# An attention and spectral-mixing kernel on one core: the weights of its issue planner set per quarter of a chunk instead of per chunk

## The chip, the core and the metric

The kernel runs on one core of one Trainium2 chip. Times are device microseconds (us) of that core. Three runs of the kernel before took 399.91, 400.09 and 401.86 us; their median is 400.09 us. The engines are called as in the profile: PE (matmuls) with PEld (its weight loads), ACT, DVE, POOL, and SP, which only issues DMAs here.

## The reference

Softmax attention over 2048 tokens (16 heads of 28) and a two-dimensional Fourier filter are computed of the same input and mixed by a gate per token.

```python
def reference(A_x, A_wqkv, A_wo, B_x, B_w_r, B_w_i, gate_w):
    def _A_ref(x, wqkv, wo):                       # x: 1 x 2048 x 448
        q, k, v = qkv[0], qkv[1], qkv[2]           # 16 heads of 28
        scores = jnp.einsum("bhqd,bhkd->bhqk", q, k) * Dh ** -0.5
        p = _softmax(scores, axis=-1)
        o = jnp.einsum("bhqk,bhkd->bhqd", p, v)
        return o.transpose(...).reshape(B, S, D) @ wo
    def _B_ref(x, w_r, w_i):
        X = jnp.fft.rfft2(x.astype(jnp.float32), axes=(-2, -1))
        y = jnp.fft.irfft2(X * (w_r + 1j * w_i), s=(S, D), axes=(-2, -1))
        return y.astype(jnp.bfloat16)
    x = A_x
    g = _sigmoid((x * gate_w).sum(-1, keepdims=True))
    a = _A_ref(x, A_wqkv, A_wo)
    b = _B_ref(x, B_w_r, B_w_i)
    return g * a + (1 - g) * b
```

## The kernel before

**The attention.** The 16 heads form four groups G of four heads; the 2048 queries form four blocks j of 512. A pair (G, j) is a *chunk*, and there are 16. Inside a chunk the keys come in 16 blocks of 128. One such block for the four heads of the group is a *pack*: 16 packs a chunk, 256 in all. Each pack needs four score matmuls (`KT` by `QT`, 128 keys x 512 queries each), an exponential of each, and four matmuls by the values (`Vb`) that add into the one PSUM bank `psV`.

**Two ways for a pack.** On the ACT way the scores go into the double banks `psA` and `psB`, two heads at a time; that pair is called a *score tile* here. ACT turns a score tile into `P` with one exponential of 128x1024 (L901), so an ACT pack takes two of them. `P` is a ring of 20 slots of 512 columns, which is ten exponentials; the first five ACT packs go into `VS` instead (`nearly=5`). On the DVE way each head's scores go into a bank `psX`, DVE turns them into the bits of an approximate exponential by an add and a maximum (L930), and three shifted copies of 128x2048 (L936) refine it; the pack then takes four passes of value matmuls instead of one. So an ACT pack costs ACT two instructions, and a DVE pack costs DVE seven.

**The rest.** Around this stream stand the projections of keys, queries and values, the norms that bound the scores (`sq`, `brow`, which goes into `QT` by DMAs), the gate (`glog`, `ge`, `gg`), the Fourier stages (`f1`, `f2`, `f3`, `i1`, `i2` by their unit names, over `UZ`, `P2`, `FX`, `t`, `Qf`), the division of each chunk by its sums (`osb`, `rs`, `rg`, `RB`, then a product on POOL, L1521) and the output projection (`out`). At the start the weights of group 0's values are exponentiated on ACT (L1227) and multiplied into `Vb` on DVE (L1348) before any value matmul may run.

**The planner.** Nothing of the order is written out by hand. `Plan.run` holds a clock for each engine and gives the engine that is furthest behind its next piece of work; the emitted program follows that order, engine by engine, and the engines then run in order with semaphores between them. For PE, `pe_step` first issues the next score tile if its bank pair is free; otherwise every other piece that is ready makes an `offer` with a score, and the lowest wins. Terms of the score are the weights: `w_pv` (value matmuls), `w_open` and `w_new` (units of background work), `w_d` (scores for a DVE pack), `w_due`, `w_late`, `w_hungry`, `sw_pen` (a change between row-tiled and column-tiled matmuls). `tol` is how late a score tile may become; `z_hard` and `z_soft` say at which PE load filler matmuls (`zero`) are added; `d_open`, `ahead`, `sh_max` and `d_urg` steer how many packs DVE claims. `step` does the same for DVE, ACT, POOL and SP by priority. Which pack goes to ACT and which to DVE falls out of this.

Progress is `next_a / 16`, the index of the next unclaimed pack in chunks, from 0 to 16, and 17 when no scores are left. The planner looks up its weights by progress.

```python
        self.cfgs = [dict(cfg, **cfg["seg"].get(i, {})) for i in range(18)]
...
            self.cfg = self.cfgs[int(self.progress())]
...
        if not any(self.s_left):
            return 17.0
        return (self.next_a if self.next_a < self.NP else self.NP) / 16.0
```

Of the kernel before, what the change touches and what calls it, by code (L numbers as in the profile page):

```python
# [111 lines left out]
class Op:  # L112
# [46 lines left out]
class Plan:  # L159
# [116 lines left out]
    def run(self):  # L276
        c = self.cfg
        self.mode = "full"
        self.owner = {b: None for b in self.banks}
        self.free_at = {b: 0.0 for b in self.banks}  # L280
        self.port_until = {"DVE": 0.0, "POOL": 0.0}
        self.marks = getattr(self, "marks", {})
        self.cells = []
        for o in self.ops:
            self.register(o)
        for u in self.units:
            for o in u.pe:
# [552 lines left out]
    def unit_run(self, u, o, t):  # L840
# [3 lines left out]
        self.pe_run(o, t)  # L844


CFG = dict(
    port_dep=6.0, last=((0, 2), (2, 2)), x_act=4, tiles=(2, 2), nring=20, nvar=10, nearly=5, l_pe=0.09, l_act=0.03, pe_lat=0.2, dma_issue=0.6,
    m_pe=0.2, m_bank=0.1, tol=0.1, max_ahead=9, nd_max=99, d_open=3, ahead=3, d_chunks=1, dve_op1=0.605, dve_shift=0.6, pool_shift=2.0,
    pool_shifts=(), pool_every=0, prio_op1=3, prio_shift=2.5, sh_max=4, d_urg=2, window=3.413, z_hard=3450, z_soft=3500, v2_at=2.0, v2_due=2.8,  # L850
    g_at=(0.9, 4.3, 8.0), g_due=1.0, w_pv=1.0, w_open=0.5, w_new=1.6, w_late=0.5, w_d=3, w_due=2, hungry=1.4, v_rush=2, x_rush=6, k_rush=5, q_rush=4,
    w_hungry=1, sw_pen=0, pv_min=1, ring_urg=2, d_first=True,
    seg={
        0: dict(d_open=4, w_hungry=0, z_hard=3550, w_open=1.2),
        1: dict(tol=0),
        3: dict(tol=0.15),
        4: dict(ahead=2, tol=0.15),
        5: dict(v2_due=3.1, hungry=4, w_pv=0.6, tol=0.15),
        6: dict(hungry=4, prio_shift=3, tol=0.15),
        7: dict(w_pv=0.6, tol=0, v2_at=0.5, prio_shift=3),  # L860
        8: dict(w_pv=0.6, tol=0, prio_shift=3, z_hard=3550),
        9: dict(d_urg=1, d_chunks=0, w_due=4, prio_shift=3, z_hard=3550),
        10: dict(z_hard=3550, d_open=4),
        11: dict(z_hard=3550, g_at=[1.1, 4.3, 8.0]),
        12: dict(d_urg=1, ring_urg=8, z_hard=3550),
        13: dict(ring_urg=4, w_pv=0.2, prio_shift=3, z_hard=3550, d_urg=1, w_new=2.0, z_soft=3800, w_late=2),
        14: dict(w_open=0.2, prio_shift=3.5, ahead=1, w_late=2, w_pv=0.2, ring_urg=4, w_new=2.0, w_due=4, pv_min=2, z_soft=3800),
        15: dict(prio_shift=3.5, w_open=0.2, w_late=1, w_pv=0.2, z_hard=3350, w_new=1.2, w_due=4, pv_min=2, z_soft=3800),
        16: dict(sw_pen=1.5),
        17: dict(z_soft=3800, w_new=1.2),  # L870
    },
)

# [69 lines left out]
class Kernel:  # L943
# [36 lines left out]
    def tiles(self, ctx):  # L980
# [629 lines left out]
```

## Time and profile before

| | |
|---|---|
| median of three runs | 400.09 us |
| the profiled execution | 400.49 us |
| its span, first to last instruction | 398.7 us |
| granted PE clock over the span | 1.000 |
| POOL busy | 126.9 us (32%) |
| DMA, mean over the span | 44 GB/s, 17.69 MB |

The span is 1.79 us shorter than the time of the same execution. In the profile's rows a column holds the start, the length, the engine, the line of the program, the operation, `out<-in`, the shapes and the count; what stands in brackets is idle time before it and what ended it. A score tile and its exponential carry the same number in the text: exponential 21 reads score tile 21.

### The profile page before, as it was taken

What the parts mean: (1) busy time and instruction counts of PE and PEld (TensorE: products, weight loads), DVE (VectorE), ACT (ScalarE), POOL (GpSimd) and SP (SyncE); (2) the same over time, 40 slices, a digit from 0 to 9 for tenths busy, and PEclk for the clock granted to TensorE, in tenths of its full rate; (3) what the DMA queues carried; (4) which work ended last, traced back from release to release, by engine and by line L of the source; (5) the groups of instructions that cost most, each with busy time, mean ns of one, the idle gap of its engine ahead of it and who ended that gap; (6) DMA issues with size and microseconds to landing.
All of it is one profiled execution on the core that took longest, in us unless ns stands there. A gap on an engine that the chain in (4) does not pass through costs nothing.

```text
span 398.7 us, 12653 instructions
## 1 busy us (share of the span) xinstructions
PE 386.0 (97%) x5221; PEld 134.9 (34%) x5221; DVE 344.3 (86%) x622; ACT 383.6 (96%) x424; POOL 126.9 (32%) x176
## 2 busy tenths in 40 slices
PE   8999999999999999999999999999999999999996
PEld 4444332223333322332332333333334332323233
DVE  3668999988887897898799797799998999999992
ACT  4898999999999999999999999999999999999993
POOL 1044214432333135525444534542436720101010
PEclk9999999999999999999999999999999999999999
DMA  8800022000121102120130112012100100001012
GB/s 250 181 31 5 2 28 58 13 19 3 37 70 34 40 3 66 32 77 20 24 100 19 56 37 58 14 42 74 36 29 2 29 3 25 30 27 50 26 53 71
DMA packets 24394, 17.69 MB, mean 44 GB/s; under 512 B 15731, under 2 KB 19744, under 8 KB 24336
## 3 DMA queue, kind: packets, MB, share of 16 engines
q1 hardware_dynamic: 23728, 16.69, 15.7%
q8 instruction: 41, 0.67, 0.7%
q10 hardware_dynamic: 608, 0.19, 0.3%
q14 instruction: 17, 0.14, 0.1%
HBM read 14.71 MB, written 1.97 MB: 42 GB/s over the span
## 4 chain that ended last, share of the span: by engine, by line
PE 46%; ACT 44%; issue 8%; DMA 1%; DVE 1%; ACTq 0%; DVEq 0%
ACT P L901 44%; PE psX L952 16%; PE psV L952 13%; PE psB L952 8%; PE psA L952 8%; DMA xtok<-in_A_x_dram 1%; PE psX L1202 1%; ACT VS L901 0%; DVE KT L1246 0%; DVE QT L1246 0%; ACT Vb L1227 0%; DVE Vb L1348 0%; PE psV L1202 0%; ACT sq L1556 0%; ACT sq L1237 0%
## 5 line engine op out<-in xcount | busy, mean ns | idle before, releaser
L901 ACT ACTIVATE P<-psB 128x1024 bf16<-128x1024 f32 x198 | 219.9, 1110 | 0.0
L901 ACT ACTIVATE P<-psA 128x1024 bf16<-128x1024 f32 x198 | 219.6, 1109 | 0.1
L930 DVE TENSOR_SCALAR VS<-psX 128x512 int16<-128x512 f32 x212 | 138.9, 681 | 17.3 <-PE psX L952 16.4
L936 DVE TENSOR_SCALAR VS<-VS 128x2048 int16<-128x2048 int16 x159 | 101.5, 689 | 0.4
L952 PEld LDWEIGHTS <-KT 32*128 32x128 bf16 (+1 forms) x1040 | 47.8, 91 | 145.3 <-issue 141.0
L952 PE MATMUL psB<-QT,KT 32*128 32x512 bf16 x406 | 79.2, 382 | 6.3 <-ACT P L901 5.0
L952 PE MATMUL psA<-QT,KT 32*128 32x512 bf16 x406 | 79.6, 383 | 0.9 <-DVE QT L1246 0.6
L952 PE MATMUL psV<-VS,Vb 128*32 128x512 bf16 x868 | 76.0, 385 | 0.1
L952 PE MATMUL psV<-P,Vb 128*32 128x512 bf16 x792 | 73.7, 385 | 0.0
L952 PE MATMUL psX<-QT,KT 32*128 32x512 bf16 x212 | 70.4, 383 | 0.0
L952 PEld LDWEIGHTS <-Vb 128*32 128x32 bf16 x1660 | 33.3, 94 | 57.0 <-issue 51.9
L1441 POOL TENSOR_TENSOR t<-FX,Wf 128x452 bf16<-128x452 f32 x32 | 31.8, 1013 | 56.1 <-PE psX L952 26.3
L1521 POOL TENSOR_TENSOR xtok<-osb,RB 128x512 bf16<-128x512 f32 x12 | 15.3, 1274 | 61.8 <-DMA RB<-rgd 47.6
L1184 POOL TENSOR_TENSOR sq<-QT 128x512 bf16<-128x512 bf16 x16 | 16.6, 1040 | 42.9 <-DVE QT L1266 17.3
L1495 POOL TENSOR_TENSOR UZ<-tab 128x225 bf16<-128x225 f32 (+1 forms) x32 | 17.7, 583 | 21.0 <-DVE VS L936 14.7
L952 PE MATMUL psX<-xT,Wk 112*32 112x512 bf16 x256 | 20.5, 383 | 0.0
L952 PE MATMUL psX<-xT,Wq 112*32 112x512 bf16 x240 | 20.0, 383 | 0.0
L1184 POOL TENSOR_TENSOR sq<-KT 128x512 bf16<-128x512 bf16 x12 | 12.5, 1040 | 22.6 <-DVE KT L1174 17.1
L952 PE MATMUL psX<-Bd,UZ 112*32 112x452 bf16 x256 | 19.6, 358 | 0.0
L1449 POOL TENSOR_TENSOR t<-t,t 128x226 bf16<-128x226 bf16 x32 | 17.9, 584 | 5.0 <-DVE VS L936 4.3
L952 PE MATMUL psX<-Wv,xT 112*32 112x113 bf16 (+1 forms) x512 | 19.4, 262 | 0.0
L952 PEld LDWEIGHTS <-xT 112*32 112x32 bf16 (+1 forms) x576 | 10.5, 96 | 9.0 <-issue 7.0
(105 smaller groups left out, 301.5 us busy)
## 6 DMA issues: line engine op xcount, KB each, us to landing
tab<-c_tab SPq DMA_DIRECT2D x16, 256.0 KB
RB<-rgd SPq DMA_DIRECT2D x60, 64.0 KB
xtok<-in_A_x_dram SPq DMA_DIRECT2D x4, 448.0 KB
out_dram<-ost SPq DMA_DIRECT2D x6, 224.0 KB
rs<-osb SPq DMA_DIRECT2D x60, 2.0 KB
Wf<-in_B_w_r_dram SPq DMA_DIRECT2D x31, 28.1 KB
Wf<-in_B_w_i_dram SPq DMA_DIRECT2D x31, 28.1 KB
Qf<-in_A_wqkv_dram SPq DMA_DIRECT2D x2, 294.0 KB
```

Of the source, the lines that this page charges most:

```text
L901: k.nc.scalar.activation(out=out, in_=k.psS[e["grp"]][:, 0:n, :], func=ACT.Exp, scale=LN2_128)
L930: k.nc.vector.tensor_scalar(out=k.VS[:, slot, 512 * h:512 * h + 512], in0=bank, scalar1=float(BITS0), scalar2=BITS_MIN, op0=ALU.add, op1=A ...
L936: k.nc.vector.tensor_scalar(out=k.VS[:, dst, :], in0=k.VS[:, src, :], scalar1=float(SHIFTS[v - 1]), scalar2=None, op0=ALU.add)
L952: self.nc.tensor.matmul(out, lhsT=lhsT, rhs=rhs, start=start, stop=stop, skip_group_check=True, **kw)
L1184: (self.nc.vector if e == "DVE" else self.nc.gpsimd).tensor_tensor(out=sq[:, :], in0=src, in1=src, op=ALU.mult)
L1202: nc.tensor.transpose(out=bb[0:C, 512 * ci + 128 * k:512 * ci + 128 * k + 128], in_=self.xtok3[:, 4 * b + k, C * c:C * c + C], identity=se ...
L1441: ts.append(pl.op("POOL", 1.07, lambda e, i=i, q=q: nc.gpsimd.tensor_tensor(out=self.t12[i][q][:, :].rearrange("p (r f) -> p r f", r=2), i ...
L1449: (nc.vector if e == "DVE" else nc.gpsimd).tensor_tensor(out=t1[:, FP * q:FP * q + FP], in0=t1[:, FP * q:FP * q + FP], in1=t2[:, FP - FP * ...
L1495: nc.gpsimd.tensor_tensor(out=z, in0=a, in1=b, op=ALU.subtract if q else ALU.add)
L1521: prev = pl.op("POOL", 1.3, lambda e, G=G, j=j: nc.gpsimd.tensor_tensor(out=self.ON[G][:, 512 * j:512 * j + 512], in0=self.osb[:, :], in1= ...
```

## The change

`GRAIN = 4` cuts each chunk into four quarters of four packs. The table of weights has 72 entries in place of 18, and each quarter has its own. Most entries of before are spread over their four quarters with further weights added.

```diff
-        self.cfgs = [dict(cfg, **cfg["seg"].get(i, {})) for i in range(18)]
+        self.cfgs = [dict(cfg, **cfg["seg"].get(i, {})) for i in range(18 * GRAIN)]
...
-            self.cfg = self.cfgs[int(self.progress())]
+            self.cfg = self.cfgs[int(GRAIN * self.progress())]
...
+GRAIN = 4
...
-        0: dict(d_open=4, w_hungry=0, z_hard=3550, w_open=1.2),
-        1: dict(tol=0),
-        3: dict(tol=0.15),
...
-        10: dict(z_hard=3550, d_open=4),
-        11: dict(z_hard=3550, g_at=[1.1, 4.3, 8.0]),
...
-        16: dict(sw_pen=1.5),
-        17: dict(z_soft=3800, w_new=1.2),
+        0: dict(d_open=4, w_hungry=0, z_hard=3550, w_open=1.2, tol=0.15, sh_max=3),
+        1: dict(d_open=4, w_hungry=0, z_hard=3350, w_open=1.2, tol=0.15, sh_max=3, w_late=4, w_d=2.2),
+        2: dict(d_open=4, w_hungry=0, z_hard=3550, w_open=1.2, tol=0.15, sh_max=3, prio_shift=3),
+        3: dict(d_open=4, w_hungry=0, z_hard=3550, w_open=1.2, ahead=6, max_ahead=5),
+        4: dict(tol=0),
...
+        40: dict(d_open=4, hungry=3, d_urg=3, sw_pen=0.25, pv_min=3),
+        41: dict(z_hard=3550, d_open=4, hungry=3, d_urg=3, sw_pen=0.25, pv_min=3),
+        42: dict(z_hard=3550, d_open=4, hungry=3, sw_pen=0.25, pv_min=3, w_new=2.0, w_due=0, ahead=2),
+        43: dict(z_hard=3550, d_open=4, hungry=3),
+        44: dict(z_hard=3550, g_at=[1.1, 4.3, 8.0], hungry=0, w_due=0.5, prio_shift=3.5),
...
+        68: dict(z_soft=3800, w_new=1.2, z_hard=3350, pv_min=3),
+        69: dict(z_soft=3800, w_new=1.2, z_hard=3350, pv_min=3),
+        70: dict(z_soft=3800, w_new=1.2, z_hard=3350, pv_min=3),
+        71: dict(z_soft=3800, w_new=1.2, z_hard=3350, pv_min=3),
```

The functions that emit instructions are the same, and every line below the table of weights moves by 56 (L901 becomes L957). What the planner makes of the new weights is seen in the two built programs, engine by engine. The counts that differ:

| instructions | before | after |
|---|---|---|
| ACT exponentials of score tiles (L901) | 406 | 404 |
| DVE bits of a head's scores (L930) | 212 | 216 |
| DVE shifted copies (L936) | 159 | 162 |
| value matmuls, four to a pass, from `P` / from `VS` | 792 / 868 | 788 / 884 |
| filler matmuls, four to a pass, into `psV` / `psX` | 8 / 12 | 32 / 0 |
| stretches of one tiling mode on PE | 787 | 794 |
| evacuation of key block 1 of group 0 (L1244, L1246) | DVE | ACT |
| one DMA queue (SP) and POOL: instructions by kind | same | same |

So one pack of 256 goes from ACT to DVE. Places in the order, counted in score tiles issued on PE or exponentials issued on ACT before them:

| place | before | after |
|---|---|---|
| ACT squares of key blocks of group 0 (L1237) | after exponentials 2, 6, 10 | 2, 4, 5 |
| ACT exponential of the value weights (L1227) | after 19 | after 14 |
| ACT exponential of the gate (L1358) | after 20 | after 26 |
| last of the first four value units on PE | tile 21 | tile 25 |
| first value matmuls from `VS` / from `P` | tile 21 / 22 | tile 18 / 20 |
| first scores of a DVE pack | tile 22 | tile 16 |
| `psV` evacuated, chunks 0 to 14, first and last | tile 33, 387 | tile 30, 383 |
| last `i1` and first `i2` | tile 295, 302 | tile 293, 295 |
| last scores of a DVE pack | 2 tiles before the last | 7 tiles before the last |

More of the change, by code (lines that the diff above doesn't have):

```diff
@@ L864 @@
-        11: dict(z_hard=3550, g_at=[1.1, 4.3, 8.0]),
[L865 to L868, printed above, removed]
-        16: dict(sw_pen=1.5),
@@ new lines @@
+        7: dict(tol=0, d_urg=0, pv_min=2),
+        8: dict(d_urg=0, z_hard=3550, w_pv=1.4),
+        9: dict(d_urg=3, hungry=1, w_new=2.4),
+        10: dict(sw_pen=2, ahead=1),
+        11: dict(pv_min=2),
+        12: dict(tol=0.15, pv_min=2, z_soft=4200, ring_urg=10),
+        13: dict(tol=0.15, pv_min=2, z_soft=4200, ring_urg=10, ahead=1),
+        14: dict(tol=0.15, pv_min=2, z_soft=4200, ring_urg=10, ahead=1),
+        15: dict(tol=0.15, pv_min=2, z_soft=4200, ring_urg=10, sh_max=2),
+        16: dict(tol=0.15, pv_min=2, z_soft=4200, ring_urg=10),
@@ new lines @@
+        17: dict(ahead=1, tol=0.15, pv_min=2, z_soft=4200, ring_urg=10, sw_pen=1),
+        18: dict(ahead=2, tol=0.15, pv_min=2, z_soft=4200, ring_urg=10, w_pv=1.8),
+        19: dict(ahead=2, tol=0.15, pv_min=2, z_soft=4200, ring_urg=10, w_pv=1.8, w_d=1, prio_shift=3.5),
+        20: dict(v2_due=3.1, hungry=4, w_pv=1.8, tol=0.15, ring_urg=10, w_d=1, prio_shift=3, sh_max=3),
+        21: dict(v2_due=3.1, hungry=4, tol=0.15, w_d=1, prio_shift=3.5, w_hungry=0, z_soft=4200),
+        22: dict(v2_due=3.1, hungry=3, w_pv=0.6, tol=0.15, w_d=1, prio_shift=3.5, z_soft=4200, d_first=False, d_urg=3),
@@ new lines @@
+        23: dict(v2_due=3.1, hungry=4, w_pv=0.6, tol=0.15, w_d=1, prio_shift=3.5, z_soft=4200, d_first=False, d_urg=3, w_due=4, ahead=4),
+        24: dict(hungry=4, tol=0.15, w_d=1.7, z_soft=4200, d_first=False, d_urg=3, w_due=4, ahead=4, sw_pen=2, w_new=0.8),
+        25: dict(hungry=4, prio_shift=3.5, tol=0.06, w_d=1, z_soft=4200, d_first=False, d_urg=3, w_due=4, ahead=4, pv_min=3, ring_urg=6),
+        26: dict(hungry=4, prio_shift=3.5, tol=0.15, w_d=1, z_soft=4200, d_first=False, d_urg=3, w_due=4, ahead=4),
@@ new lines @@
+        27: dict(hungry=4, prio_shift=3.5, tol=0.15, w_d=1, z_soft=4200, d_first=False, d_urg=3, w_due=4, ahead=6, ring_urg=10),
+        28: dict(w_pv=0.6, tol=0, v2_at=0.5, prio_shift=3, z_soft=4200, d_first=False, hungry=3, d_urg=3, ring_urg=10, ahead=6),
+        29: dict(w_pv=0.6, tol=0, v2_at=0.5, z_soft=4200, hungry=3),
+        30: dict(w_pv=0.6, tol=0, v2_at=0.5, prio_shift=3, z_soft=4200, d_first=False, hungry=3, d_urg=3, w_due=0),
+        31: dict(w_pv=0.6, tol=0, v2_at=0.5, prio_shift=3, z_soft=4200, d_first=False, hungry=1, d_urg=3),
@@ new lines @@
+        32: dict(w_pv=0.6, prio_shift=3, z_soft=4200, d_first=False, hungry=1, d_urg=3, sw_pen=0.25),
+        33: dict(w_pv=0.6, prio_shift=3, z_soft=4200, hungry=1, d_urg=3, sw_pen=2),
+        34: dict(w_pv=0.6, prio_shift=3, z_soft=4200, hungry=3, d_urg=3, sw_pen=2, w_late=2),
+        35: dict(w_pv=0.6, prio_shift=3, hungry=3, d_urg=3, sw_pen=0.25),
+        36: dict(d_urg=3, d_chunks=0, w_due=4, prio_shift=3, hungry=4, sw_pen=0.25, w_new=0.8, w_hungry=2),
+        37: dict(d_urg=3, d_chunks=0, w_due=4, prio_shift=3, hungry=3, sw_pen=0.25, max_ahead=5),
@@ new lines @@
+        44: dict(z_hard=3550, g_at=[1.1, 4.3, 8.0], hungry=0, w_due=0.5, prio_shift=3.5),
+        45: dict(z_hard=3550, g_at=[1.1, 4.3, 8.0], hungry=0, w_due=0.5, prio_shift=3.5, sw_pen=0.25),
+        46: dict(z_hard=3550, g_at=[1.1, 4.3, 8.0], sw_pen=0.5),
+        47: dict(z_hard=3550, g_at=[1.1, 4.3, 8.0], sw_pen=0.25, d_first=False),
+        48: dict(d_urg=1, ring_urg=8, z_hard=3550, sw_pen=0.5, w_new=2.4),
+        49: dict(d_urg=1, ring_urg=8, z_hard=3250, sw_pen=0.5),
+        50: dict(d_urg=1, ring_urg=8, z_hard=3250, sw_pen=0.5),
@@ new lines @@
+        51: dict(d_urg=1, ring_urg=8, z_hard=3550, sw_pen=0.5, z_soft=4200, ahead=5, pv_min=3),
+        52: dict(ring_urg=4, w_pv=0.2, prio_shift=3, z_hard=3550, d_urg=1, w_new=2.4, z_soft=4200, ahead=5, pv_min=3),
+        53: dict(ring_urg=4, w_pv=0.2, prio_shift=3, z_hard=3550, d_urg=1, w_new=2.4, z_soft=4200, ahead=5, pv_min=3, w_d=0.5, hungry=2),
+        54: dict(ring_urg=4, w_pv=0.2, prio_shift=3, z_hard=3550, d_urg=1, w_new=2.4, z_soft=3800, w_d=0.5, ahead=5, hungry=2, d_first=False),
@@ new lines @@
+        55: dict(ring_urg=4, w_pv=0.2, prio_shift=3, z_hard=3550, d_urg=1, w_new=2.4, z_soft=3800, w_late=2, tol=0, sh_max=1),
+        56: dict(w_open=0.2, prio_shift=3.5, ahead=1, w_late=2, w_pv=0.2, ring_urg=4, w_new=2.4, w_due=4, pv_min=2, z_soft=3800, z_hard=3350),
+        57: dict(prio_shift=3.5, ahead=1, w_late=2, w_pv=0.2, ring_urg=4, w_new=2.0, w_due=4, z_soft=3800, z_hard=3350, d_urg=0),
+        58: dict(prio_shift=3.5, ahead=1, w_late=2, w_pv=0.2, ring_urg=4, w_new=2.0, w_due=4, z_soft=3800, z_hard=3350, d_urg=0),
```

19 lines of the change are left out of this document (13 added, 6 removed).

## The prediction

> **What bounds the kernel now.** I read the page first: its table of engines, then the chain.
>
> ```profile
> span 398.7 us, 12653 instructions
> PE 386.0 (97%) x5221; PEld 134.9 (34%) x5221; DVE 344.3 (86%) x622; ACT 383.6 (96%) x424; POOL 126.9 (32%) x176
> ...
> PE 46%; ACT 44%; issue 8%; DMA 1%; DVE 1%; ACTq 0%; DVEq 0%
> ```
>
> PE and ACT look equally full and the chain passes between them, so neither view says which sets the pace. The groups, and then the exponentials from number 21 on as instructions of one line, do.
>
> ```profile
> L901 ACT ACTIVATE P<-psA 128x1024 bf16<-128x1024 f32 x198 | 219.6, 1109 | 0.1
> L952 PE MATMUL psB<-QT,KT 32*128 32x512 bf16 x406 | 79.2, 382 | 6.3 <-ACT P L901 5.0
> L901 ACT ACTIVATE P<-psA x193: 1017/1105/1290, 34.7 to 387.3; 128x1024 bf16<-128x1024 f32 x193
> L901 ACT ACTIVATE P<-psB x193: 1017/1098/1292, 35.6 to 388.2; 128x1024 bf16<-128x1024 f32 x193
> ```
>
> ACT is almost never idle before an exponential, while PE waits 5.0 us for ACT before score tiles. The timeline of ACT gives the pace.
>
> ```profile
> 12.65 1.02 ACT L901 ACTIVATE VS<-psA 128x1024 bf16<-128x1024 f32 x1 [1.10 <-PE psB L952]
> ...
> 14.96 1.04 ACT L901 ACTIVATE VS<-psA 128x1024 bf16<-128x1024 f32 x1
> ...
> 17.67 1.08 ACT L901 ACTIVATE VS<-psB 128x1024 bf16<-128x1024 f32 x1
> 18.57 0.67 ACT L1237 ACTIVATE sq<-psX 128x512 bf16<-128x512 f32 x1
> 19.05 1.10 ACT L901 ACTIVATE VS<-psA 128x1024 bf16<-128x1024 f32 x1
> ...
> 30.41 1.23 ACT L901 ACTIVATE P<-psA 128x1024 bf16<-128x1024 f32 x1
> 31.33 0.65 ACT L1227 ACTIVATE Vb<-psX 128x64 bf16<-128x64 f32 x1
> 31.44 1.40 ACT L901 ACTIVATE P<-psB 128x1024 bf16<-128x1024 f32 x1
> 34.35 0.21 ACT L1358 ACTIVATE ge<-glog 128x16 f32<-128x16 f32 x1 [1.51 <-DVE glog L1334]
> 34.71 1.02 ACT L901 ACTIVATE P<-psA 128x1024 bf16<-128x1024 f32 x1
> ...
> 388.22 1.04 ACT L901 ACTIVATE P<-psB 128x1024 bf16<-128x1024 f32 x1
> ```
>
> From 14.96 to 17.67 are three steps of 0.903 (the durations overlap): call 0.905 the floor. From exponential 21 (34.71) to 406 (388.22) the 385 steps take 353.51, or 0.918 each, 1.4% above the floor: ACT bounds this stretch. So the span is a sum along ACT: 12.65 to the first exponential, 22.06 for 20 steps, 353.51 for 385, 1.04 for the last, 9.44 behind it (398.70 - 389.26). At the floor the 20 steps would take 18.10. Three squares among them cost 0.475 each (17.67 to 19.05 is 1.38), together 1.43. The step from 31.44 is 3.27, or 2.37 too long. The 0.16 left is mostly L1227, whose step is 1.03.
>
> What that step of 3.27 waits for stands on PE and DVE.
>
> ```profile
> 33.03 0.39 PE L952 MATMUL psB<-QT,KT 32*128 32x512 bf16 x2
> ...
> 33.35 1.05 PE L952 MATMUL psV<-VS,Vb 128*32 128x512 bf16 x16
> 34.23 1.25 PE L952 MATMUL psV<-P,Vb 128*32 128x512 bf16 x20
> ...
> 32.02 1.70 DVE L1348 TENSOR_TENSOR Vb<-Vb 128x448 bf16<-128x448 bf16 x3 [1.22 <-ACT Vb L1227]
> ...
> 34.16 0.15 DVE L1334 COPY glog<-psX 128x4 f32<-128x4 f32 x1
> ```
>
> Two things are late at once. Exponential 21 is the first to overwrite a slot of the ring, so the ring's first pack must have had its value matmuls; those start at 34.23, behind tile 22, since `Vb` is weighted only from 32.02 on, right behind L1227. And the gate's exponential, placed ahead of 21, waits for `glog`, which leaves DVE at 34.16 behind the same work.
>
> **The change part by part, along that sum.**
>
> *Until the first exponential: 0.* One more group of 8 transposes stands ahead of score tile 1, where PE waits 0.58 us for a DVE result whose place does not change, and takes the place of a filler:
>
> ```profile
> 12.23 0.39 PE L952 MATMUL psA<-QT,KT 32*128 32x512 bf16 x2 [0.58 <-DVE QT L1246]
> ```
>
> *The first 20 steps: -1.65 with the gate's exponential.* The squares cost ACT the same 1.43 wherever they stand. L1227 moves from behind exponential 19 to behind 14: 12.65 + 14 x 0.905 + 1.43 + 0.48 (the added evacuation, below) = 27.2 in place of 31.33. DVE starts weighting 0.69 later as before (32.02 - 31.33), at 27.9, and by its order does five more pieces of up to 0.6 until the second weighting is done, at 30.3 at most. The first matmuls from `P` stand behind tile 20; its bank comes free with exponential 18, at 31.0, and a change of mode (33.03 to 33.35: 0.32) and three passes of 0.22 (33.35 to 34.23: four in 0.88) end near 32.2. Exponential 21 is due near 32.8 (12.65 + 18.10 + 1.43 + 0.48 + 0.12): 0.6 to spare. The gate's exponential now stands behind 26, at 38.2 or later; the last `glog` follows value matmuls behind tile 25, whose bank comes free at 35.5; with the change of mode, the matmuls and two pieces on DVE that is about 37.1. Both are then in time, by 0.6 and 1.1 us, and I see nothing that is late next; the 2.37 goes. The gate's exponential itself still costs something: at least what L1227 costs its step (1.03 - 0.905 = 0.12), at most 0.36 (34.35 to 34.71). So 2.01 to 2.25, and I take 2.13.
>
> Against it: one key block's evacuation (L1244, an Identity of 128x512 from PSUM) moves to ACT. No Identity runs on ACT in this trace; the nearest row is the square of the same shape, 0.475, and I take 0.48. It is 0 if ACT would have waited for tile 5 anyway, and 0.67, the square's whole duration, if nothing overlaps it. DVE loses the same work. 2.13 - 0.48 = 1.65.
>
> The Trainium skill (ScalarE: Activation LUTs, section What ACT_TABLE_LOAD costs) says that each per-partition pointer operand of an activation adds about 93 ns, and this Identity has such a bias where the square has none. By that rule it would cost 0.57 and the part 1.56. No row of before shows it.
>
> *Two exponentials fewer: -1.84.* 2 x 0.918; 1.81 at the floor. The pack they leave goes to DVE:
>
> ```profile
> L936 DVE TENSOR_SCALAR VS<-VS 128x2048 int16<-128x2048 int16 x159 | 101.5, 689 | 0.4
> 387.06 1.90 DVE L936 TENSOR_SCALAR VS<-VS 128x2048 int16<-128x2048 int16 x3
> ```
>
> Three shifts span 1.90, so one occupies (1.90 - 0.69) / 2 = 0.60; seven instructions (a bits instruction counted alike) are 4.2 us of DVE, which was busy 344.3 of 398.7. PE gains three passes of value matmuls, three of fillers and seven changes of mode at 0.10 (0.32 - 0.22): 0.66 + 0.66 + 0.70 = 2.0. Summing every pass of the built orders at such steps, 20 score tiles carry at most 18.15 us of PE work before and 18.19 after, against 18.36 for 20 exponentials, so ACT covers it; without that cover it costs the 2.0.
>
> *The other 383 steps: 0.* Their excess of 0.013 a step is spread evenly. A calm and a busy stage bound it:
>
> ```profile
> L901 ACT ACTIVATE P<-psA x20: 1051/1086/1237, 181.6 to 216.3; 128x1024 bf16<-128x1024 f32 x20
> ...
> L901 ACT ACTIVATE P<-psB x20: 1017/1025/1067, 329.2 to 364.3; 128x1024 bf16<-128x1024 f32 x20
> ```
>
> 38 steps take 34.7 (0.913) in one and 35.1 (0.924) in the other: over 383 steps -1.9 or +2.1. I take no change, since the PE work per 20 tiles is alike. Each ring slot is released with at least one tile to spare in the new order; before, only the stall above had less. On SP the same DMAs stand nearly in the same order: of group 1's four `QT` rows three now stand behind one store of `rg`, with 14 score tiles until they are read (17 before). POOL's work is the same.
>
> *Behind the last exponential: 0.*
>
> ```profile
> 389.43 0.39 PE L952 MATMUL psV<-P,Vb 128*32 128x512 bf16 x4
> ```
>
> The last pass starts 0.17 after that exponential ends, and what follows it is the same list. The DVE packs end earlier in the order, which can free 0.1 at most.
>
> **Sum.** -1.65 - 1.84 = -3.49. Against the profiled execution, 400.49 (span 398.70 and 1.79 around it): 397.0. That execution stood 0.40 above the median of the runs shown, so for the median 400.09 - 3.49 = 396.6.
>
> **Rivals.** *The stall moves (398.7).* If `glog` or the ring is late again, the 2.13 stays: -1.84 + 0.48 = -1.36. For: it was a wait on hardware that the order did not foresee; against: the margins of 0.6 and 1.1 us above.
>
> *DVE takes over in a stretch (398.4).* Counted at 0.60 a piece, the new order gives DVE 37.4 us of work over score tiles 260 to 300 (32.7 before), where 40 exponentials need 36.7. If PE then waits for DVE packs, the moved pack returns its 1.8. Against: from tile 260 to the end DVE has 124.5 us of work in 132.2, so the backlog of 0.7 clears.
>
> *Late evacuations of `psV` (405.6, the slower side).* One bank takes all value matmuls, and each chunk's first must wait for one DVE copy:
>
> ```profile
> L1512 DVE COPY osb<-psV 128x512 f32<-128x512 f32 x15 | 10.2, 679 | 0.0
> ```
>
> With DVE fuller, each of the 15 may queue behind one more piece of 0.60 with PE at a standstill: +9.0, so 400.09 - 3.49 + 9.0. From 10 such delays on the kernel is over 0.5% slower. Against: most ring slots leave five tiles or more of slack, and DVE's fullest stages before show no gap on ACT.
>
> *PE's clock drops (403.6).* It is 1.00 throughout:
>
> ```profile
> PEclk9999999999999999999999999999999999999999
> ```
>
> At half clock a pass takes 0.43 for 0.22, and 20 score tiles with 16 us of PE work need some 25, about 7 more than ACT: -3.49 + 7. The emptiest four tiles hold the columns of 3456 full-array cycles before (tile 288) and 3594 after (tile 351), so nothing gets emptier. The Trainium skill (TensorE: Matmul & The Clock Gate, Part 1) says that an idle window of about 3.4 us halves the clock; nothing here has shown one.
>
> *The middle tightens (394.7).* All steps as in the calm stage: -1.9.
>
> **How the numbers follow.** The forecast, 395.0 to 398.0 as its own range, gets 0.55; the stall moved 0.13; DVE's stretch 0.10; late evacuations 0.08; the clock 0.04; the tighter middle 0.10. Over 0.5%, 2.0 us, counts as a difference, so faster means under 398.1: 0.55 + 0.10 + half of DVE's case = 0.70. Same: 0.13 + 0.05 = 0.18. Slower: 0.12. The range 394.7 to 400.0 leaves out those 0.12 and the lower half of the tighter middle, 0.05.
>
> **What would show it.** 404 exponentials, the last ending near 385.8 in a span near 395.2; exponential 21 at 32.8 with no step over 1.5 us behind it; a mean step of 0.918 from there; 9.4 us behind the last. An idle ACT ahead of `ge` or 21 shows the first rival, DVE rows without gaps with PE waiting for them the second, gaps of PE ahead of value matmuls ended by `osb` the third. I am wrong if the mean step leaves 0.913 to 0.924.

## The result, and the profile after

The changed kernel takes **397.78 us** (median of ten runs, 397.10 to 399.75); beside it the kernel before took 400.64 us (ten runs, 399.91 to 402.34). The ratio is 0.9934, with an interval of 0.9911 to 0.9958: faster by about 2.6 us. The forecast was 396.6 us with 395.0 to 398.0 as its own range. The profiled execution took 397.11 us with a span of 395.3.

The page of the changed kernel, its span, its engines and its chain of waits:

```profile
span 395.3 us, 12706 instructions
PE 384.1 (97%) x5244; PEld 131.4 (33%) x5244; DVE 347.0 (88%) x628; ACT 382.7 (97%) x423; POOL 127.5 (32%) x176
...
PE 51%; ACT 39%; issue 7%; DVE 1%; DMA 1%; SPq 0%; DVEq 0%; ACTq 0%
```

Both engines stay at 97%, but the chain has shifted: before it ran 46% over PE and 44% over ACT, now 51% and 39%. The steps of ACT that run long are more: behind exponential 21, 18 of them exceed 1.0 us, where before 10 did. The groups and the exponentials out of `psB` from number 20 on, as instructions of one line, give the rest:

```profile
L1008 PE MATMUL psB<-QT,KT 32*128 32x512 bf16 x404 | 78.6, 383 | 4.2 <-ACT P L957 3.4
L957 ACT ACTIVATE P<-psB x193: 1017/1086/1292, 31.6 to 385.3; 128x1024 bf16<-128x1024 f32 x193
```

PE waited 5.0 us for ACT ahead of score tiles in `psB` before, and 3.4 us now. The timeline of ACT in the changed kernel (start, length, engine, line, operation) has the places that the prediction named:

```profile
12.13 1.02 ACT L957 ACTIVATE VS<-psA 128x1024 bf16<-128x1024 f32 x1 [1.09 <-PE psB L1008]
13.05 1.02 ACT L957 ACTIVATE VS<-psB 128x1024 bf16<-128x1024 f32 x1
...
14.43 1.04 ACT L957 ACTIVATE VS<-psA 128x1024 bf16<-128x1024 f32 x1
15.34 1.06 ACT L957 ACTIVATE VS<-psB 128x1024 bf16<-128x1024 f32 x1
16.24 0.72 ACT L1300 ACTIVATE KT<-psX,onef 128x512 bf16<-128x512 f32 x1
...
17.29 1.08 ACT L957 ACTIVATE VS<-psA 128x1024 bf16<-128x1024 f32 x1
...
31.60 1.28 ACT L957 ACTIVATE P<-psB 128x1024 bf16<-128x1024 f32 x1
32.68 1.12 ACT L957 ACTIVATE P<-psA 128x1024 bf16<-128x1024 f32 x1
...
37.34 1.05 ACT L957 ACTIVATE P<-psB 128x1024 bf16<-128x1024 f32 x1
38.26 0.22 ACT L1414 ACTIVATE ge<-glog 128x16 f32<-128x16 f32 x1
38.36 1.03 ACT L957 ACTIVATE P<-psA 128x1024 bf16<-128x1024 f32 x1
...
385.31 1.02 ACT L957 ACTIVATE P<-psB 128x1024 bf16<-128x1024 f32 x1
```

The stall is gone: the step into exponential 21 (31.60 to 32.68) is 1.08 where it was 3.27, and the gate's exponential at 38.26 waits for nothing. The last exponential ends at 386.33 (385.31 + 1.02), half a microsecond behind the 385.8 of the forecast, and the way there has other sizes than the sum had. The table divides both spans at exponential 27, since the gate's exponential now stands behind 26; in the kernel before it starts here:

```profile
40.25 1.03 ACT L901 ACTIVATE P<-psA 128x1024 bf16<-128x1024 f32 x1
```

| part of the span | before | after | difference | forecast |
|---|---|---|---|---|
| to the first exponential | 12.65 | 12.13 | -0.52 | 0 |
| exponentials 1 to 27, with the gate's | 27.60 | 26.23 | -1.37 | -1.65 |
| exponentials 27 to the last | 347.97 (379 steps) | 346.95 (377 steps) | -1.02 | -1.84 |
| from the start of the last | 10.48 | 9.98 | -0.50 | 0 |
| span | 398.70 | 395.29 | -3.41 | -3.49 |

Two steps fewer at 0.918 are -1.84, so the remaining 377 steps lost 0.82. The sum over the span came out within 0.1, because a loss of 0.8 in the middle and one of 0.3 at the head stand against a gain of 1.0 at the two ends that no step of the prediction contains.

### The profile page after: what moved, and what is told of

The parts are those of the page before. It is cut to its first block, busy times and chain, and to the rows that moved or that the text cites. A ratio compares the mean times of both kernels' runs of the same rounds, so it can differ in the third digit from the quotient of the medians.

```text
span 395.3 us, 12706 instructions
## 1 busy us (share of the span) xinstructions
PE 384.1 (97%) x5244; PEld 131.4 (33%) x5244; DVE 347.0 (88%) x628; ACT 382.7 (97%) x423; POOL 127.5 (32%) x176
## 4 chain that ended last, share of the span: by engine, by line
PE 51%; ACT 39%; issue 7%; DVE 1%; DMA 1%; SPq 0%; DVEq 0%; ACTq 0%
ACT P L957 37%; PE psX L1008 17%; PE psV L1008 15%; PE psB L1008 9%; PE psA L1008 8%; ACT VS L957 1%; DMA xtok<-in_A_x_dram 1%; DVE VS L992 1%; PE psX L1258 0%; SPq L1160 0%; DVE KT L1302 0%; DVE QT L1302 0%; DVE VS L986 0%; ACT sq L1612 0%; ACT sq L1293 0%
## 5 line engine op out<-in xcount | busy, mean ns | idle before, releaser
L957 ACT ACTIVATE P<-psA 128x1024 bf16<-128x1024 f32 x197 | 216.1, 1097 | 0.1
L957 ACT ACTIVATE P<-psB 128x1024 bf16<-128x1024 f32 x197 | 215.7, 1095 | 0.1
L986 DVE TENSOR_SCALAR VS<-psX 128x512 int16<-128x512 f32 x216 | 141.8, 682 | 10.9 <-PE psX L1008 9.7
L992 DVE TENSOR_SCALAR VS<-VS 128x2048 int16<-128x2048 int16 x162 | 103.8, 693 | 0.5
L1008 PEld LDWEIGHTS <-KT 32*128 32x128 bf16 x1040 | 46.1, 91 | 143.8 <-issue 141.0
L1008 PE MATMUL psV<-P,Vb 128*32 128x512 bf16 x788 | 72.6, 385 | 0.0
L1008 PEld LDWEIGHTS <-Vb 128*32 128x32 bf16 x1672 | 31.9, 94 | 57.0 <-issue 53.9
L1008 PE MATMUL psX<-xT,Wk 112*32 112x512 bf16 x256 | 19.1, 383 | 0.0
```

The costliest lines, as they stand in the source:

```text
L957: k.nc.scalar.activation(out=out, in_=k.psS[e["grp"]][:, 0:n, :], func=ACT.Exp, scale=LN2_128)
L986: k.nc.vector.tensor_scalar(out=k.VS[:, slot, 512 * h:512 * h + 512], in0=bank, scalar1=float(BITS0), scalar2=BITS_MIN, op0=ALU.add, op1=A ...
L992: k.nc.vector.tensor_scalar(out=k.VS[:, dst, :], in0=k.VS[:, src, :], scalar1=float(SHIFTS[v - 1]), scalar2=None, op0=ALU.add)
L1008: self.nc.tensor.matmul(out, lhsT=lhsT, rhs=rhs, start=start, stop=stop, skip_group_check=True, **kw)
```

## The experiments

Times are medians, but for the two rows marked as profiled; each ratio is against runs of the kernel before on the same chip. "Middle" is the time from exponential 21 to the last, and "mean step" that time over the number of steps; these two and the start of 21 come from the one profiled execution of each kernel.

| kernel | exponentials | us | ratio and interval | start of 21 behind the first | middle, mean step |
|---|---|---|---|---|---|
| before (profiled) | 406 | 400.49 | | 22.06 | 353.5, 0.918 |
| changed (profiled) | 404 | 397.11 | 0.9934 (0.9911 to 0.9958) | 20.54 | 352.6, 0.921 |
| new weights in chunk 0 only | 410 | 404.22 | 1.0103 (1.0090 to 1.0117) | 20.54 | 357.9, 0.920 |
| old weights in chunk 0 only | 410 | 407.80 | 1.0203 (1.0179 to 1.0227) | 22.06 | 360.2, 0.926 |
| at most 50 DVE packs | 412 | 405.31 | 1.0128 (1.0113 to 1.0144) | 20.55 | 360.6, 0.922 |
| gate's exponential late | 406 | 408.26 | 1.0203 (1.0184 to 1.0223) | 22.06 | 353.6, 0.918 |
| ring of 22, gate late | 408 | 405.97 | one run | 19.87 | 357.6, 0.924 |
| 12 more fillers | 404 | 398.04 | 0.9947 (0.9932 to 0.9962) | 20.54 | 353.6, 0.923 |
| 47 more fillers | 404 | 403.83 | 1.0093 (1.0076 to 1.0109) | 20.71 | 358.2, 0.935 |
| 20 more shifts on DVE | 404 | 406.12 | 1.0157 (1.0093 to 1.0221) | 20.55 | 362.6, 0.947 |
| key block 1 on DVE | 404 | 396.96 | 0.9920 (0.9905 to 0.9935) | 20.41 | 352.5, 0.920 |
| no fillers | 404 | 397.09 | 0.9906 (0.9877 to 0.9935) | 20.55 | 352.3, 0.920 |
| no fillers, key block 1 on DVE | 404 | 397.52 | 0.9919 (0.9895 to 0.9942) | 20.41 | 352.7, 0.921 |
| no fillers, again (six executions; the profiled one took 415.14 us) | 404 | 397.94 | 0.9936 (0.9915 to 0.9958) | 20.54 | 370.4, 0.967 |

### Chunk 0 alone, and everything but chunk 0

In the first kernel the new quarters 0 to 3 stand over the old weights of all other chunks; in the second it is the other way round. The second's edit of the changed kernel:

```diff
-        0: dict(d_open=4, w_hungry=0, z_hard=3550, w_open=1.2, tol=0.15, sh_max=3),
-        1: dict(d_open=4, w_hungry=0, z_hard=3350, w_open=1.2, tol=0.15, sh_max=3, w_late=4, w_d=2.2),
...
+        0: dict(d_open=4, w_hungry=0, z_hard=3550, w_open=1.2),
+        1: dict(d_open=4, w_hungry=0, z_hard=3550, w_open=1.2),
...
```

> The new weights in the four quarters of chunk 0 alone, the old ones of before in every other quarter. The planner then makes 410 exponentials of score tiles (before 406, after 404), with L1227's place behind 14 and the gate's behind 26 as in the new kernel. Theory (ACT sets the pace; the head's stall is a gain of its own): 4 exponentials more at 0.918 are +3.7 us, the head gives -1.4, so 2.3 us over before, about 402.9; exponential 21 starts 20.5 us behind the first one, as in the new kernel. Rival A (the count of exponentials does not matter, PE sets the pace): 1.4 under before, 399.2. Rival B (what the head gains is lost again further on): as head_old within 0.3.

> The old weights in the four quarters of chunk 0, the new ones everywhere else; also 410 exponentials, and L1227 and the gate's exponential behind 19 and 20 as before. Theory: no gain at the head, +3.7 us for four exponentials: 404.3; exponential 21 starts 22.0 us behind the first. It is 1.4 slower than head_new, which has as many. Rival A (PE sets the pace): 400.6, as before. Rival B (the head's gain is lost further on): within 0.3 of head_new.

The head follows chunk 0's weights exactly: exponential 21 starts 20.54 behind the first where they are new and 22.06 where they are old, whatever comes later. The time does not: both halves of the change are slower than either whole, since either makes the planner claim 410 exponentials. Six more than the changed kernel are 5.5 us at 0.918. The head is therefore worth 1.5 us, and the rest of the gain exists only for the particular plan of all 72 entries. Both forecasts of the time were too low: 402.9 for the first kernel, 404.3 for the second. In the first profile 1.8 us of that is a later first exponential (14.46 against 12.65); in the second the middle is 3.0 us longer than four more exponentials make it, and most of this is one step.

The second kernel also shows the third rival once. At one change of chunk (ACT, PE and DVE rows of the kernel with old weights in chunk 0) the copy out of `psV` stands behind three shifts:

```profile
147.56 1.89 DVE L992 TENSOR_SCALAR VS<-VS 128x2048 int16<-128x2048 int16 x3
...
149.37 0.69 DVE L1568 COPY osb<-psV 128x512 f32<-128x512 f32 x1
...
150.11 0.40 PE L1008 MATMUL psV<-P,Vb 128*32 128x512 bf16 x4 [0.73 <-DVE osb L1568]
...
150.60 1.02 ACT L957 ACTIVATE P<-psA 128x1024 bf16<-128x1024 f32 x1 [1.84 <-PE psV L1008]
```

DVE finishes the shifts first, PE waits 0.73 for the copy, and ACT 1.84 for the ring slots that the late value matmuls read. The step is 2.91 in place of 0.905, so the price was 2.0 us, more than the 0.60 of the prediction. It was paid at one of fifteen changes of chunk here. In the changed kernel PE waits once for such a copy too, 0.30 at 278.37, and the next steps of ACT stay at the floor.

### Fewer DVE packs

```diff
-    ... nd_max=99, d_open=3, ...
+    ... nd_max=50, d_open=3, ...
```

> The new kernel with at most 50 packs for DVE (54 there), so 412 exponentials in place of 404; DVE has 16.8 us less to do and PE twelve passes of value matmuls less. Theory (ACT sets the pace): +8 x 0.92 = 7.4 us over the new kernel, about 405.1, with the mean step of the exponentials still 0.918 to 0.921. Rival (PE or DVE shares the pace, so relief there comes back as a shorter step): under 402, with the mean step at 0.910 or less.

405.31 us for 412 exponentials: eight more cost 7.5 us, 0.94 each. What an exponential is worth is right. The mean step is 0.922, a little over the 0.918 to 0.921 expected; 0.5 of the middle lies in the two steps behind exponential 71, of which the run without fillers below tells more. With 16.8 us less for DVE the steps did not become shorter. PE was hardly relieved: it has twelve passes of value matmuls fewer, but the planner made 18 filler passes in place of 8.

### What held exponential 21

```diff
-            ..., func=ACT.Exp, scale=-1.0), self.o_g, prio=-1)
+            ..., func=ACT.Exp, scale=-1.0), self.o_g + [self.o_u[4]], prio=-1)
```

> Before, with the gate's exponential made to wait for the fifth Fourier evacuation: it then stands behind exponential 27 in place of 20; L1227 stays behind 19, 406 exponentials. Theory (the ring alone holds exponential 21 until the first value matmuls are done): exponential 21 still starts 21.8 to 22.1 us behind the first, and the time is that of before within 0.5. Rival (the wait for glog alone made the stall): 20.0 behind the first and 2 us less, 398.6.

The kernel before, with the gate's exponential behind exponential 27. Its timeline of ACT:

```profile
33.09 1.40 ACT L901 ACTIVATE P<-psB 128x1024 bf16<-128x1024 f32 x1
36.37 1.02 ACT L901 ACTIVATE P<-psA 128x1024 bf16<-128x1024 f32 x1 [1.88 <-PE psV L952]
```

The step is 3.28, as before, with the gate out of the way, and the wait now bears PE's value matmuls into `psV` as its end. The time, forecast within 0.5 of the kernel before, came out 8 us longer. Of the 8.8 us of the profiled execution, 1.7 are a later first exponential, and 7.1 lie at the end: the planner left output units behind the last exponential, and from the end of that one the tail takes 16.5 us (9.4 before).

With the same edit of the gate, and two slots more:

```diff
-    ... nring=20, ...
+    ... nring=22, ...
```

> The kernel before with two more slots in the ring (22 of 512 columns, eleven exponentials) and the gate's exponential put behind exponential 28, so that only the ring can hold ACT near exponential 21. The planner replans: 408 exponentials, so its time is not compared. If the stall of 2.37 at exponential 21 is the ring's first reuse, it is gone from 21 (start 19.7 behind the first in place of 22.06) and comes back at 22, the first to overwrite a slot now, shorter by the one exponential of 0.9 that fits in, about 1.5. If the stall was anything else in front of 21, it stays at 21 with 22.06.

```profile
32.89 1.23 ACT L901 ACTIVATE P<-psA 128x1024 bf16<-128x1024 f32 x1
35.53 1.02 ACT L901 ACTIVATE P<-psB 128x1024 bf16<-128x1024 f32 x1 [1.40 <-PE psV L952]
```

With one exponential more in the ring the stall leaves 21 (19.87 behind the first in place of 22.06) and comes back at 22 with a step of 2.64, which is 1.7 over the floor where 1.5 was expected. It is the ring's first reuse. The gate's wait, which the prediction named beside it, ended at the same moment and cost nothing of its own; how long it would hold ACT alone was not tried.

### How much of PE's work comes through

Fillers of zero weights are added behind the value matmuls of every 16th (every 4th) pack of the ACT way; they add nothing to the sums.

```diff
+        self.na = getattr(self, "na", 0) + 1
+        if self.na % 16 == 0 and not x.last:
+            self.zero("col", None, False)
```

> The changed kernel with twelve more passes of filler matmuls (zero weights, added into psV), one behind the value matmuls of every 16th pack that ACT exponentiated; nothing else moves. Each pass is 0.22 us of PE work, 2.6 us in all. Theory A (PE work between score tiles hides behind the exponentials, as the prediction had it): mean step from exponential 21 stays at 0.9207 within 0.001, time within 0.4 us of the changed kernel's. Theory B (about half of each added microsecond of PE work comes through, as 2.0 us more gave 0.96 in the changed kernel): middle longer by 1.3, mean step 0.924. If all came through it would be 2.6.

> The changed kernel with 47 more passes of filler matmuls, one behind the value matmuls of every 4th pack that ACT exponentiated: 10.2 us of PE work. PE work per score tile rises from 0.884 to 0.911, just above the floor of 0.905 of an exponential. Theory A: the middle grows only where 20 tiles carry more than 18.36 us, 2 us at most. Theory B: about half comes through, 5 us, mean step 0.934. If the whole kernel were bound by PE it would be 10.2.

Twelve passes (2.6 us of PE) make the middle longer by 1.02, and 47 (10.2 us) by 5.59: 39% and 55% come through. The trace with 47 more lacks a collision of POOL and DVE that the changed kernel has at 76 us (shown below), and its two steps there are 0.44 shorter; without these two it is 6.02, or 59%.

How it happens, in the kernel with twelve more (PE and ACT):

```profile
74.45 0.39 PE L1011 MATMUL psV<-cst 128*32 128x512 bf16 x4
74.77 0.39 PE L1011 MATMUL psA<-QT,KT 32*128 32x512 bf16 x2
...
74.09 1.11 ACT L957 ACTIVATE P<-psB 128x1024 bf16<-128x1024 f32 x1
75.26 1.02 ACT L957 ACTIVATE P<-psA 128x1024 bf16<-128x1024 f32 x1
```

The filler at 74.45 puts off the score tile behind it by 0.22, and the exponential that reads this tile starts 1.17 behind its forerunner instead of 0.96. PE has no idle time here: between these two score tiles it simply has more work than one exponential lasts. Seven of the 383 steps rose by 0.08 to 0.22 and one fell by 0.17; behind the other fillers ACT was the late one, and they cost nothing. With only two score tiles of depth, an average over 20 tiles hides this.

### How much of DVE's work comes through

```diff
-            k.nc.vector.tensor_scalar(out=k.VS[:, dst, :], in0=k.VS[:, src, :], ...)
+            self.ns = getattr(self, "ns", 0) + 1
+            for _ in range(2 if self.ns % 8 == 0 else 1):
+                k.nc.vector.tensor_scalar(out=k.VS[:, dst, :], in0=k.VS[:, src, :], ...)
```

> The changed kernel with every 8th shifted copy on DVE issued twice (the second writes the same values again): 20 copies, 12 us of DVE work at 0.60, and no other change. If DVE has slack wherever ACT packs run beside it, as its 88% of busy time says, 0 to 1 us. If the middle's lost microsecond is DVE being late in the fullest stretches (the prediction's second rival), 4 us or more, with PE waiting for VS ahead of value matmuls and DVE rows without gaps there. If evacuations of psV queue behind it (third rival), single steps of 1.5 us and more at the changes of chunk, up to 9 us in all.

Twelve microseconds of DVE made the middle 10.0 longer in the profiled execution (407.88 us); the other three took 404.03, 404.37 and 409.71. Of the 10.0, 3.9 are lost in the six steps behind exponential 70. PE, then ACT, then the windows (busy us of PE, PEld, DVE, ACT and POOL, and the clock granted to PE):

```profile
79.88 0.40 PE L1010 MATMUL psV<-VS,Vb 128*32 128x512 bf16 x4 [1.01 <-DVE VS L994]
...
80.71 1.02 ACT L957 ACTIVATE P<-psA 128x1024 bf16<-128x1024 f32 x1 [0.93 <-PE psA L1010]
...
78.20:81.60 3.40, 2.24 (x27) 0.66 (x24) 3.37 (x6) 2.47 (x3) 1.08 (x1) 1.00 0.22 63
81.60:88.40 6.80, 6.80 (x50) 1.14 (x47) 5.65 (x11) 4.23 (x5) 2.31 (x2) 0.50 0.04 12
```

PE waits 1.01 for the shifts (four here with the doubled one, 3.33 us in all beside POOL's product), and 1.7 us later its clock falls to one half for 6.8 us, in which ACT is busy 4.23. Two rivals of the prediction in a row: DVE is late, then the clock drops. That the one brought on the other is not shown. In the two shortest executions the granted clock was 1.000 throughout, so DVE without the clock costs about half of what is added to it (404.2 against 397.8 for 12 us).

### The evacuation that moved to ACT

```diff
-                    o.emit() if eng == "PE" else o.emit(eng)
+                    o.emit() if eng == "PE" else o.emit("DVE" if eng == "ACT" and o.alt == "ACT" and o.name == "k0" else eng)
```

> The changed kernel with the evacuation of key block 1 of group 0 put back from ACT to DVE at the same place of the order. If that Identity costs ACT what its step shows, exponential 21 starts 0.57 earlier behind the first (19.97 in place of 20.54), and the time is 0.57 under the changed kernel's, 0.48 by the prediction's term. If ACT would have waited there anyway, exponential 21 stays at 20.54 and the step holds an idle stretch ended by PE or DVE in place of the instruction.

In the changed kernel the step around it (15.34 to 17.29) is 1.95. An exponential and a square take 1.38 (13.05 to 14.43), so the Identity costs 0.57 and not the 0.48 of the square. The Trainium skill (ScalarE: Activation LUTs, section What ACT_TABLE_LOAD costs) has 93 ns for each pointer operand; 0.48 + 0.09 is what the trace shows. With the evacuation on DVE the same steps read:

```profile
15.40 1.05 ACT L957 ACTIVATE VS<-psB 128x1024 bf16<-128x1024 f32 x1
16.69 0.60 ACT L1293 ACTIVATE sq<-psX 128x512 bf16<-128x512 f32 x1 [0.23 <-ACT VS L957]
17.18 1.02 ACT L957 ACTIVATE VS<-psA 128x1024 bf16<-128x1024 f32 x1
...
16.19 0.40 PE L1008 MATMUL psX<-xT,Wk 112*32 112x512 bf16 x4
```

Only 0.17 comes back in this step (1.78) and 0.13 by exponential 21. The square now waits for key block 2, whose matmuls run at 16.19 on PE and end at 16.59 with or without the edit; the bracket names ACT, whose exponential had ended at 16.45. So 0.44 of the 0.57 lay in time that ACT would have waited anyway. Both expectations missed: the step holds an idle stretch ended by PE, and a small gain as well.

### The fillers taken out

```diff
+        if bank is None and not first:
+            return
```

> The changed kernel without its 8 filler passes into psV (32 matmuls with zero weights, which add nothing to the result); the order is otherwise the same. They are 8 x 0.217 = 1.7 us of PE work. Theory A (PE hides behind the exponentials): no change, mean step 0.9207. Theory B (40 to 55% of PE work comes through, as twelve and 47 added passes gave): middle shorter by 0.7 to 1.0, mean step about 0.9185, time 0.7 to 1.0 under the changed kernel's. The fillers' own purpose, theory C: without them the granted clock falls to 0.5 in some stretch of the emptiest tiles, with exponentials 0.7 us and more late there, and several us lost.

The middle is 0.37 shorter, less than theory B had. Step by step against the changed kernel, all of it lies in the two steps behind exponential 71 (-0.41 together); the others are the same within 0.12 and cancel. The fillers that were taken out stood at 45.3, 273.5 and later, none of them near. In the changed kernel stand here, on ACT, DVE and POOL:

```profile
78.66 1.10 ACT L957 ACTIVATE P<-psA 128x1024 bf16<-128x1024 f32 x1
79.76 1.02 ACT L957 ACTIVATE P<-psB 128x1024 bf16<-128x1024 f32 x1
...
76.15 2.73 DVE L992 TENSOR_SCALAR VS<-VS 128x2048 int16<-128x2048 int16 x3
...
75.15 1.05 POOL L1430 TENSOR_TENSOR R1s<-omg,cst 128x512 bf16<-128x512 bf16 x1 [1.46 <-DMA omg<-gd]
76.16 1.57 POOL L1240 TENSOR_TENSOR sq<-QT 128x512 bf16<-128x512 bf16 x1
...
78.93 0.40 PE L1008 MATMUL psV<-VS,Vb 128*32 128x512 bf16 x4 [0.17 <-DVE VS L992]
```

and in the kernel without fillers:

```profile
76.57 1.89 DVE L994 TENSOR_SCALAR VS<-VS 128x2048 int16<-128x2048 int16 x3
...
74.57 1.05 POOL L1432 TENSOR_TENSOR R1s<-omg,cst 128x512 bf16<-128x512 bf16 x1 [0.89 <-DMA omg<-gd]
75.57 1.04 POOL L1242 TENSOR_TENSOR sq<-QT 128x512 bf16<-128x512 bf16 x1
```

Three shifts take 1.89 alone and 2.73 beside POOL's product; the product takes 1.57 in place of 1.04. Started within 0.01 of each other, each waits for the other in the changed kernel; by the lengths, POOL for the first shift and then a later shift for POOL. PE then waits 0.17 for `VS` and brings its score tiles late, 0.41 on ACT. In the kernel without fillers POOL had started 0.6 earlier, since the DMA into `omg` landed earlier; the shifts start 0.42 later there and still end 0.42 earlier. The Trainium skill (SBUF — State Buffer, section Who interferes with whom) says that such copies on VectorE and GpSimd's instructions share one pair of ports as an exclusive lock, and that the later one blocks fully; these rows agree. The two steps are long in the traces with twelve more fillers, with 50 DVE packs and with key block 1 on DVE as well. With 47 more fillers the same product took 2.83 and the three shifts 1.88: there POOL bore the loss alone, and ACT lost nothing.

> The changed kernel without the 8 filler passes and with key block 1's evacuation on DVE: the two edits together as a candidate for the faster kernel. If they add up: 0.13 from the first 21 exponentials and 0.7 to 1.0 from the middle, so 396.7 against 397.5 to 397.8. If the clock falls, it is slower than the changed kernel, as for the run without fillers alone.

Without the fillers and with the evacuation on DVE: 397.52 us where 396.7 was expected, and the two steps bear the collision again (a shift of 1.53 in the trace). So the gain of 0.41 does not come of the missing fillers; what decides where the DMA lands was not settled.

> The kernel without the 8 filler passes once more, in more rounds, to tell what its shorter middle came from. In its first profile the whole gain (0.41 of 0.37) lies in the two steps behind exponential 71, where POOL's product L1242 (sq from QT) started at 75.57, ahead of the shifted copies of DVE, and not at 76.16 together with them as in the changed kernel. If that start is a matter of the run (it hangs on a DMA into omg, which landed 0.6 earlier), the steps may be 1.10 and 1.15 again in this profile, and the median stays within 0.5 of the changed kernel's. If it comes of the missing fillers, the steps are 0.90 and 0.93 again and the start 13.5 behind exponential 54.

The profiled execution of this run answers another question than the one asked. It took 415.14 us; the other six, from which the ratio is made, took 396.77 to 398.95. The granted clock on its page, then its windows:

```profile
PEclk9999755569999999999999999999999999999999
```

```profile
45.00:46.00 1.00, 0.46 (x7) 0.19 (x4) 1.00 (x4) 1.00 (x3) 0.00 (x0) 1.00 0.03 2
46.00:90.00 44.00, 43.81 (x301) 10.46 (x300) 26.75 (x48) 29.50 (x30) 9.70 (x10) 0.51 0.10 20
```

The same window of the changed kernel:

```profile
45.00:46.00 1.00, 0.81 (x10) 0.36 (x9) 1.00 (x4) 1.00 (x2) 0.00 (x0) 1.00 0.03 2
```

and of the first profile without fillers (396.58 us):

```profile
45.00:46.00 1.00, 0.48 (x6) 0.15 (x5) 1.00 (x4) 1.00 (x2) 0.00 (x0) 1.00 0.03 2
```

PE is busy 0.46 of the microsecond from 45 to 46, where the changed kernel has its first filler and 0.81; just behind it the clock falls to one half for 44 us, with 25 steps of 1.5 us and more on ACT. That would fit theory C of the run before, in which this filler guards the emptiest place. But the other profile has the same microsecond just as empty, and its clock stayed at 1.00; and it is one execution of seventeen without fillers, of which the other sixteen took 396.58 to 398.96. Theory C is not shown: a drop that has nothing to do with the fillers isn't excluded. The question about POOL stays without an answer from this run.

## Why the prediction came out

- **What bounds the kernel: right, but too simple.** The sum along ACT holds in every run: 404 to 412 exponentials, about 0.92 each. What it misread is the 1.4% above the floor, which it took to be spread evenly. In the trace before, 41 of the 385 steps exceed 0.95 and hold 3.29 of the 5.08 us above 0.905; in the changed kernel 42 of 383 hold 4.19 of 6.02. The loss sits in single steps; what held each of them was traced for a few only.
- **The stall goes: right; one of its two reasons was idle.** Exponential 21 was forecast at 32.8 and starts at 32.68; that this is early comes of the first exponential, and counted from it the forecast was 20.13 and the trace has 20.54. The ring alone made the stall. The matmuls from `P` were to end near 32.2 and the gate's logits to be there near 37.1; by the rows of PE and DVE they end at 32.26 and 37.30. The step at 21 keeps 0.17 over the floor.

```profile
31.65 0.61 PE L1008 MATMUL psV<-P,Vb 128*32 128x512 bf16 x8
32.19 0.39 PE L1008 MATMUL psA<-QT,KT 32*128 32x512 bf16 x2
...
37.15 0.15 DVE L1390 COPY glog<-psX 128x4 f32<-128x4 f32 x1
```

  The score tile that exponential 21 reads is the one at 32.19, right behind those matmuls: a wait that the prediction's 0.6 to spare did not count.
- **The head's size: -1.65 forecast, -1.37 measured.** The Identity is 0.57 (0.48 assumed), the gate's exponential 0.12 (0.24 assumed: 37.34 to 38.36 is 1.02), the rest of the step at 21 0.17; some 0.14 lies in single steps around them.
- **Two exponentials fewer: right.** The kernel with 412 confirms the price.
- **The other steps: 0 was the step that failed.** They cost 0.82, inside the bound of +2.1. The prediction's "so ACT covers it", drawn from the load of 20 tiles, is wrong in kind: PE's added work is paid where neighbouring score tiles carry more of it than their exponentials last, as in the step shown, and 39 to 59% of it came through in the test kernels. About half of the 0.82 is the collision of POOL and DVE at 76 us (0.41). Of the 2.0 us counted for PE, the three filler passes cost nothing by the run without them; the three value passes and seven changes of mode, 1.36 together, stand against the other 0.41. That these are the cause is argued from the rate, not shown by taking them out alone; and taking work out did not pay at that rate, since the eight fillers returned 0.01 outside the two steps at 76 us.
- **Behind the last, and ahead of the first: 0 forecast, -0.50 and -0.52 measured.** Kernels with the same head order reach the first exponential anywhere from 12.06 to 14.46, and the -0.52 comes of the first sixteen transposes, the same in both orders, which last 1.95 in the trace before and 1.10 in the one after (last section). Of the -0.50, 0.44 lies behind ACT's last cast, where only the stores of the output are left; these casts stand 5.42 and 5.41 behind the last value matmuls (389.43 and 386.47). So the order accounts for 0.06 of it, and the rest of both was luck. The casts, before and after:

```profile
394.85 0.53 ACT L1556 CAST sq<-psX 128x448 bf16<-128x448 f32 x1 [0.41 <-PE psX L952]
```

```profile
391.88 0.53 ACT L1612 CAST sq<-psX 128x448 bf16<-128x448 f32 x1 [0.41 <-PE psX L1008]
```

- **The rivals.** The stall did not move. DVE does not take over in the changed kernel between 260 and 300 tiles; it is late once, at 76 us, by a cause that the prediction did not have. A late copy of `psV` cost 2.0 us once in a test kernel, and ACT nothing here. The clock stays at 1.000 in the changed kernel, but two of the test kernels lost it for a stretch, each shortly behind a microsecond in which PE was half idle or more; a third trace has such a microsecond (0.48) and kept the clock.
- **The total.** -3.49 against -2.64 by the ratio (0.0066 x 400.09), whose interval, -1.68 to -3.56, just holds the forecast. The parts that the order explains in the traces are -1.37, -1.02 and -0.06, or -2.45: 0.28 short at the head and 0.82 in the middle. That the span of the profiled execution met the sum within 0.1 is the luck of its ends.

No kernel tried here is faster than the changed one beyond the intervals: key block 1 on DVE stands at 0.9920, and no fillers at 0.9906 and, again, at 0.9936.

## What to carry to other kernels

Average load hides what single tiles pay: with two score tiles in flight, add up the feeding engine's work between neighbouring tiles, not over twenty. Of what was added on PE here, 39 to 59% was lost. That a deeper buffer would cover it was not tried. Weights of a planner are one object: half of a good set planned six exponentials more and lost 6 to 10 us against the whole. Before a filler is removed because it costs nothing, look at what the clock does in more than a few runs.

## What the runs showed of the hardware

- **The clock fell without an empty stretch ahead of it.** The 3.4 us ahead of the drop hold 2.24 us of busy PE (78.20 to 81.60, with 20 more shifts). The Trainium skill (TensorE: Matmul & The Clock Gate, Part 1) has it fall after an idle window of about 3.4 us and come back after a busy one; here it fell without an idle window, and stayed at one half for 44 us with PE busy 43.81 of them (without fillers, in the execution of 415.14 us). PE's share of busy time does not tell when: from 42.60 to 46.00 it was 2.86 us in that execution and 2.68 in the one of 396.58 us, which kept its clock.
- **Two engines with short instructions can each lose half a microsecond by starting together** (76.15 and 76.16: the product 1.57 in place of 1.04, the three copies 2.73 in place of 1.89).
- **The start differs by 2 us between executions** with the same order there. The kernel before, the changed kernel, then the one with new weights in chunk 0 only (the first twelve of its sixteen), on PE:

```profile
4.82 1.95 PE L1202 MATMUL psX<-cst,xtok 128*112 128x128 bf16 x16
```

```profile
4.77 1.10 PE L1258 MATMUL psX<-cst,xtok 128*112 128x128 bf16 x16 [0.40 <-DMA xtok<-in_A_x_dram]
```

```profile
5.72 1.53 PE L1254 MATMUL psX<-cst,xtok 128*112 128x128 bf16 x12 [1.02 <-DMA xtok<-in_A_x_dram]
```

In the third the input lands 0.95 later than in the second, and the transposes run at 0.13 each instead of 0.07; their first exponentials start at 14.46 and 12.13. In the first they start at once as in the second and take 0.12 each; both lengths occur with either order (1.10 with the ring of 22, 1.96 with no fillers and key block 1 on DVE). The granted clock reads 1.00 in all three, so the rows do not tell why.
